# Chunk 2 of a layernorm, an MLP and a long convolution enters without transposes, and GpSimd makes each first tap product

## The chip, the cores and the metric

The kernel runs on one core of one Trainium2 chip. The metric is device time in microseconds (us), from the start of the program to its end. Engines are named as in the profile: PE is TensorE (PEld its weight loads), DVE is VectorE, ACT is ScalarE, POOL is GpSimd, SP is SyncE, which only issues DMAs here.

## The reference

A sequence of 2048 rows of 448 channels goes through two branches that are added to the input. Branch A is a short causal convolution of `k` (4 taps), a product with `v`, a long causal convolution per channel by FFT, and a gate. Branch B is a dense layer, Mish, and a dense layer back.

```python
def _A_ref(q, k, v, shift_k, ssm_k, ssm_D):
    ...
    for t in range(ks):
        k_shift = k_shift + k_pad[:, t:t + S, :] * shift_k[:, ks - 1 - t][None, None, :]
    kv = k_shift * v
    ...
    y = (lambda x, s, axes=(-2,-1): jnp.fft.irfft2(x, s=s, axes=axes))(y_f, (1, L), axes=(1, 2))[:, 0, :S, :]
    y = y + kv * ssm_D[None, None, :]
    return q * y

def _B_ref(x, w1, b1, w2):
    h = jnp.einsum("bsd,df->bsf", x, w1) + b1
    sp = jnp.log1p(jnp.exp(-jnp.abs(h))) + jnp.where(h > 0, h, jnp.zeros_like(h))
    act = h * jnp.tanh(sp)
    return jnp.einsum("bsf,fd->bsd", act, w2)

x = A_q
xn = _layernorm(x, axis=-1)
return x + _A_ref(xn, A_k, A_v, A_shift_k, A_ssm_k, A_ssm_D) + _B_ref(xn, B_w1, B_b1, B_w2)
```

## The kernel before, in words

**The MLP sets the beat.** The rows are cut into 8 chunks of 256 (numbered 0 to 7), the 1792 hidden features into 7 pairs of 128. One (chunk, pair) is a pair step, 56 in all, and each is two half steps. In the even half step of pair step i, `g1_mm` (line 556) multiplies the chunk's normalised, transposed rows by the first weights. In the odd one ACT applies Mish (line 564), ACT rounds the result to a high part `ach` (line 98), DVE makes the low part `acl` (line 99), and PE multiplies the pair step i-2 by the second weights (`g2_mm`, lines 588 to 590). Weights, rows and activations are split in such high and low parts, and three products replace one of full precision. Half step s therefore belongs to pair step s/2; chunk c starts at half step 14c.

**How a chunk enters.** `XH` and `XL` hold a chunk's normalised rows with channels on partitions. Chunks below `NT` are normalised in rows (`ln_stats`: statistics on DVE, lines 442 to 448; the power and the normalisation on POOL, lines 451 and 455), turned by PE transposes (line 508, four of 128x128 for each half `jj` of a chunk) and split (lines 520 and 518). Chunks from `NT` on come by another way. `xT_load` (line 470) loads rows that were transposed beforehand, as `xn`. `nt_stats` (lines 478 to 483) makes the statistics with six ACT instructions on the row-wise copy `qt` and two POOL instructions, and POOL stores them to DRAM (`MR`, line 486). `nt_row` (line 489, issued by SP) reads them back, spread over all partitions, into `con`; `nt_norm` (line 495) subtracts and multiplies on DVE; `nt_split` (lines 502 and 503) makes `XH` and `XL`. The half steps of these stand in `NT_AT`, `NT_SOON`, `NT_HOW` and `NT_STATS`. `con` and `xn` have one buffer each.

**The convolution lies between.** It is three stages of small DFT products. The first (`f1_mm`, line 166) takes 8 groups of the filter (`h`) and 8 groups of `kv`. Each is called a visit here: PE makes 16 small products into the two PSUM tiles `pq` and `pr`; ACT copies `pr` (line 172); DVE adds and subtracts (line 176, twice, "the folds"); the sums go to DRAM on the ACT queue (line 187). The next visit writes `pq` and `pr` again, so it needs the folds to be done. `H_AT` and `KV_AT` give each visit's half step. A group of `kv` is made by `taps`: product u of four (u = 0 on line 209 and u = 2 on line 202, whole groups; u = 1 and 3 on lines 212 and 214, two halves), each added to the sum (line 219), and the product with `v` (line 222). `taps(g, u)` is placed by the distance to the group's visit; u = 2 is already made by POOL (`taps_pool`), placed right behind the visit before. DVE makes u = 0. In this document kv0 to kv7 are the groups of `kv`, and h0 to h7 those of the filter.

**What sets the order.** It is written out by hand: `at(slot, ...)` puts work ahead of a half step's products and `after(slot, ...)` behind them. Every engine and every DMA queue goes through its list in that order, and waits on semaphores where it needs another's work. Nothing is rearranged. SP issues all loads of `k`, `v`, `hT`, `q`, the transposed rows, the rows of statistics and the stores of finished chunks (line 615) on one queue.

Of the kernel before, what the change touches and what calls it, by code (L numbers as in the profile page):

```python
# [14 lines left out]
S, D, F = 2048, 448, 1792  # L15
# [7 lines left out]

G2_LAG = 2
H_HEAD = 1
H_AT = {2: 6, 3: 9, 0: 12, 4: 16, 5: 20, 6: 26, 7: 32}
KV_AT = (24, 29, 34, 39, 44, 50, 56, 60)
POOL_H = {20: (0, 2)}
OCT_AT = (66, 3)
I2_AT = {100: ((6, 7, 0, 1), 92, (95, 97, 98, 99), (0, 2, 0, 1)),  # L30
         108: ((2, 3, 4, 5), 101, (104, 105, 106, 107), (0, 1, 0, 1))}
LATE = 2
NT = 3
NT_AT = {"q": -5, "x": -1, "stats": -2, "flush": 0, "row": (4, 8), "norm": (7, 10), "split": (8, 11)}
NT_SOON = dict(NT_AT, row=(4, 5), norm=(4, 7), split=(6, 8))
NT_HOW = {c: dict(NT_SOON) for c in (4, 7)}
NT_HOW[6] = dict(NT_AT, row=(4, 10), norm=(8, 11), split=(9, 13))
NT_HOW[7]["x"] = 0
NT_HOW[3] = dict(NT_SOON, q=-9, stats=-3, flush=-2)
NT_HOW[5] = dict(NT_AT, q=-8, stats=-4, flush=-2)  # L40
NT_STATS = {3: 27, 4: 41, 5: 53, 6: 70, 7: 82}
EVAC_SOON = 2,
G1_SOON = (69, 75, 81, 87, 89)
END = 288
# [6 lines left out]
def tile_kernel(ctx: ExitStack, tc, q, qT, k, v, sk, hT, sD, head, w1, w2, c_g, c_gi, c_i2, out):  # L51
    nc = tc.nc
    V = nc.vector
# [24 lines left out]
    E = dp.tile([NJ * 4, 64, D], F32, name="E")  # L78
    MR = {c: dp.tile([2, CH], F32, name="MR") for c in range(NT, NCHUNK)}

# [8 lines left out]
    def rs(c):  # L89
        return rstd[:, 2 * c:2 * c + 2] if c < NT else mv[:, 2 * c:2 * c + 2, 1]  # L90

# [29 lines left out]
    def dv(n=1):  # L121
        for _ in range(n):
            if drip:
                drip.pop(0)()
# [4 lines left out]
    def at(slot, fn, *args):  # L129
        plan.setdefault(int(slot), []).append((fn, args))  # L130

    def after(slot, fn, *args):
        plan2.setdefault(int(slot), []).append((fn, args))
# [4 lines left out]
    skb = sp1.tile([128, 4, D], F32, name="skb")  # L138
    HT, KR, VT, KV, PP, PS, ST, SD = {}, {}, {}, {}, {}, {}, {}, []

    def xt():
        return sp1.tile([128, 2, D], F32, name="x", bufs=7)
# [61 lines left out]
    def taps(g, u):  # L204
        if (g, u) in PP:
            o = PP.pop((g, u))
        elif u % 2 == 0:
            o = xt()
            V.tensor_mul(o, KR[g - u // 2], skb[:, u:u + 1].to_broadcast([128, 2, D]))
        else:  # L210
            o = xt()
            V.tensor_mul(o[:, 0], KR[g - (u + 1) // 2][:, 1], skb[:, u])
            dv()
            V.tensor_mul(o[:, 1], KR[g - u // 2][:, 0], skb[:, u])
        dv()
        if u == 0:
            KV[g] = o
        else:
            V.tensor_add(KV[g], KV[g], o)  # L219
            dv()  # L220
        if u == 3:
            V.tensor_mul(KV[g], KV[g], VT.pop(g))
            dv()
# [207 lines left out]
    def xn_tile():  # L431
        return mp.tile([128, 4, CH], F32, name="xn", bufs=1)

    def ln_parts(c):
        st = mp.tile([128, 2, 6], F32, name="bst", bufs=2)
        ve = mp.tile([128, 2], F32, name="ve", bufs=2)
        if c < NT:
            XN[c] = xn = xn_tile().rearrange("p a b -> p (a b)").rearrange("p (j d) -> p j d", j=2)
        eng = nc.gpsimd if 0 < c < NCHUNK - 1 else V

        def stats(jj):
            V.bn_stats(st[:, jj], Q[c][:, jj])

        def aggr(jj):
            V.bn_aggr(mv[:, 2 * c + jj], st[:, jj])

        def eps(a, b):
            V.tensor_scalar(ve[:, a:b], mv[:, 2 * c + a:2 * c + b, 1], EPS, None, op0=ALU.add)

        def power(a, b):  # L450
            nc.gpsimd.tensor_tensor(rs(c)[:, a:b], ve[:, a:b], mhalf[:, a:b], op=ALU.pow)

        def norm(jj):
            j = 2 * c + jj
            eng.tensor_scalar(xn[:, jj, :D], Q[c][:, jj], mv[:, j, 0:1], rs(c)[:, jj:jj + 1],
                              op0=ALU.subtract, op1=ALU.mult)

        def tail(a, b, copy=eng.tensor_copy):
            copy(xn[:, a:b, D:], xn[:, a:b, D - 64:D])

        return stats, aggr, eps, power, norm, tail, ve
# [60 lines left out]
    def ln_T(c, jj):  # L522
        if jj == 0:
            dv(len(drip))
            x_tiles(c)
        p = pg()
        transposes(c, jj, p)
        for lo in range(2):
            x_split(c, jj, p, lo)
# [87 lines left out]
    def mlp_slot(s):  # L617
# [3 lines left out]
        if half == 0:  # L621
            if i < n:
                c, p = pairs[i]
                if c + 1 < NT:
                    if p == 0:
# [9 lines left out]
        else:  # L635
            if i < n:
                c, p = pairs[i]
                if p == NP - 2 and c + 1 < NT:
                    ln_T(c + 1, 0)
# [14 lines left out]

    for g, t in H_AT.items():
        if g != H_HEAD:
# [10 lines left out]
    for g in range(-2, 0):  # L667
        at(12, k_load, g)
    for g, t in enumerate(KV_AT):
        d = t - (KV_AT[g - 1] if g else t - 6)  # L670
        at(t - d - (3 if g > 1 else 2), k_load, g)
        at(t - d - 1, v_load, g)
        for u in range(4):
            after(t - (2 if g else 1) - d + d * u / 4, taps, g, u)
        at(t, f1_mm, KV, g, "kv")
        if g + 1 < NO:
            after(t, taps_pool, g + 1, 2)
        after(t, f1_fold, g, "kv")
        (at if t % 2 or g == NO - 1 else after)(t + (3 if g < NO - 1 else 2), f1_out, Dkv, g, "kv")
# [43 lines left out]

    for c in range(NT, NCHUNK):
        at_ = NT_HOW.get(c, NT_AT)
        b = 2 * NP * (c - 1) + (1 if c < 5 else 0)
        at(b + at_["q"], ln_load, c)
        at(b + at_["x"], xT_load, c)
        after(NT_STATS[c], nt_stats, c)
        for jj in range(2):  # L730
# [30 lines left out]
    stats, aggr, eps, power, norm, tail, ve = ln_parts(0)  # L761
# [134 lines left out]
```

## Time and profile before

| | |
|---|---|
| time, median of 3 runs (lowest, highest) | 357.84 us (356.28, 359.15) |
| the profiled execution: its time, its span | 356.18 us, 354.4 us |
| PE busy | 349.8 us, 99% of the span |
| DVE, ACT, POOL busy | 282.1, 160.7, 72.6 us (80%, 45%, 20%) |
| moved by DMA | 83.27 MB |
| granted PE clock | 0.998 |

The profile is of one execution. Each row of a timeline gives the start, the duration, the engine, the line, the operation with out<-in, the size and the number of instructions; in square brackets stands idle time before it and what ended it. A group's row gives the number of instructions, the busy time in us with the mean in ns, and the idle time before them. All times of place below are us from the span's start. Between half steps 12 and 60 the PE takes about 2.5 us for a half step and 1.1 us for a visit.

### The profile page before, as it was taken

Reading aid. Unit: us, or ns where it says so; the run is one execution under the profiler, and the core shown is the slowest. Engines: PE = TensorE matmul, PEld = TensorE weight load, DVE = VectorE, ACT = ScalarE, POOL = GpSimd, SP = SyncE. Lnnn points to the kernel's source line nnn. Section 1 sums busy time; section 2 is a strip of 40 time slices with the busy share of each in tenths; the row PEclk is TensorE's granted clock in tenths of the full one; section 3 lists DMA queues with packets and bytes.
Section 4 is the critical chain, followed back from the end, with each engine's and each line's share of the span. In section 5 each row is a group of like instructions: output and inputs, shape, how many; then the busy total and the mean of one; then the engine's idle time right before and its main releaser. Section 6 shows DMA issues by size and latency. Waiting matters only on the chain.

```text
span 354.4 us, 7525 instructions
## 1 busy us (share of the span) xinstructions
PE 349.8 (99%) x3098; PEld 288.6 (81%) x3098; DVE 282.1 (80%) x375; ACT 160.7 (45%) x310; POOL 72.6 (20%) x85
## 2 busy tenths in 40 slices
PE   8999999999999999999999999999999999999996
PEld 2988888888888989889887568658757699979795
DVE  5899748998999998979539869868985963788943
ACT  5967552347343643364232732423724333354480
POOL 3046002822220250212000120110310116040030
PEclk9999999999999999999999999999999999999999
DMA  7999977848769356652969489679756467989076
GB/s 251 366 339 353 401 277 182 338 131 236 212 178 314 128 150 176 219 163 36 298 187 365 149 307 298 229 243 372 263 144 254 105 173 261 407 334 277 25 116 143
DMA packets 30835, 83.27 MB, mean 235 GB/s; under 512 B 3153, under 2 KB 15954, under 8 KB 30802
## 3 DMA queue, kind: packets, MB, share of 16 engines
q1 hardware_dynamic: 21986, 47.78, 39.8%
q0 software_dynamic: 4928, 22.95, 20.4%
q10 hardware_dynamic: 3888, 12.08, 12.5%
q8 instruction: 24, 0.39, 0.4%
q14 instruction: 9, 0.07, 0.1%
HBM read 54.34 MB, written 28.45 MB: 234 GB/s over the span
## 4 chain that ended last, share of the span: by engine, by line
PE 97%; DMA 1%; SPq 0%; DVE 0%; issue 0%
PE pg L556 24%; PE pg L590 13%; PE pg L588 13%; PE pg L589 13%; PE pa L556 6%; PE pq L556 5%; PE pq L166 4%; PE pa L310 3%; PE pr L556 3%; PE pr L255 3%; PE pq L255 3%; PE pp L556 2%; PE pa L255 1%; DMA x<-in_head_dram 1%; PE pp L364 1%; PE pb L556 1%
## 5 line engine op out<-in xcount | busy, mean ns | idle before, releaser
L588 PE MATMUL pg<-w2h,ach 128*128 128x448 f32 x222 | 80.7, 363 | 0.0
L590 PE MATMUL pg<-w2h,acl 128*128 128x448 f32 x222 | 80.6, 363 | 0.0
L589 PE MATMUL pg<-w2l,ach 128*128 128x448 f32 x222 | 80.5, 362 | 0.0
L99 DVE TENSOR_TENSOR acl<-a,ach 128x512 fp32r<-128x512 f32 x56 | 38.9, 694 | 33.0 <-ACT ach L98 32.8
L556 PE MATMUL pg<-XH,w1h 128*128 128x256 f32 x264 | 52.7, 283 | 0.0
L564 ACT ACTIVATE a<-pg,b1t 128x256 f32<-128x256 f32 x66 | 27.8, 472 | 51.8 <-PE pg L556 40.9
L556 PEld LDWEIGHTS pg<-XH,w1h 128*128 128x128 f32 x264 | 41.3, 188 | 8.2 <-issue 6.3
L588 PEld LDWEIGHTS pg<-w2h,ach 128*128 128x128 f32 x222 | 41.6, 187 | 4.4 <-issue 1.4
L589 PEld LDWEIGHTS pg<-w2l,ach 128*128 128x128 f32 x222 | 41.7, 188 | 2.4
L590 PEld LDWEIGHTS pg<-w2h,acl 128*128 128x128 f32 x222 | 41.7, 188 | 2.4
L556 PE MATMUL pg<-XL,w1h 128*128 128x256 f32 x264 | 42.9, 277 | 0.0
L176 DVE TENSOR_TENSOR st<-pq,st 128x896 f32<-128x896 f32 x32 | 34.9, 1089 | 4.8 <-ACT st L172 4.2
L98 ACT CAST ach<-a 128x512 fp32r<-128x512 f32 x56 | 34.8, 621 | 8.2 <-PE pg L589 6.7
L556 PEld LDWEIGHTS pg<-XL,w1h 128*128 128x128 f32 x264 | 35.9, 188 | 0.0
L556 PE MATMUL pg<-XH,w1l 128*128 128x256 f32 x198 | 33.5, 278 | 0.0
L202 POOL TENSOR_TENSOR x<-kr,skb 128x896 f32<-128x896 f32 x8 | 17.0, 2128 | 72.1 <-PE pr L166 25.7
L321 POOL DMA_DIRECT2D E<-qe x14 | 8.8, 631 | 92.7 <-ACT qe L264 92.7
L556 PEld LDWEIGHTS pg<-XH,w1l 128*128 128x128 f32 x198 | 27.6, 188 | 0.0
L219 DVE TENSOR_TENSOR x<-x 128x896 f32<-128x896 f32 x24 | 26.2, 1091 | 1.1 <-POOL x L202 0.4
L172 ACT COPY st<-pr 128x896 f32<-128x896 f32 x16 | 14.5, 908 | 15.9 <-PE pr L166 14.7
L564 ACT ACTIVATE a<-pa,b1t 128x256 f32<-128x256 f32 x16 | 6.7, 472 | 20.8 <-PE pa L556 20.7
L166 PE MATMUL pq<-x,con 32*64 32x448 f32 x128 | 15.9, 560 | 0.1
(191 smaller groups left out, 645.8 us busy)
## 6 DMA issues: line engine op xcount, KB each, us to landing
Dkv<-st ACTq DMA_DIRECT2D x16, 448.0 KB, 5.5
ah<-Dh SPq DMA_DIRECT2D x8, 896.0 KB, 8.4
av<-Dkv SPq DMA_DIRECT2D x8, 896.0 KB, 9.6
e<-E POOLq DMA_DIRECT2D x8, 896.0 KB, 7.3
E<-qe POOLq DMA_DIRECT2D x14, 448.0 KB, 7.1
kr<-in_k_dram SPq DMA_DIRECT2D x10, 448.0 KB, 6.0
Dh<-st ACTq DMA_DIRECT2D x10, 448.0 KB, 6.9
x<-in_v_dram SPq DMA_DIRECT2D x8, 448.0 KB, 6.3
```

The source lines that it names most:

```text
L98: nc.scalar.copy(h, raw)
L99: V.tensor_sub(l, raw, h)
L166: nc.tensor.matmul(ps[h][64 * jj:64 * jj + 64, b, :D], f1[rg:rg + 32], x[rg:rg + 32, jj], start=True, stop=True, tile_position=(rg, 64 * jj))
L176: f(st[:, n], e, st[:, 1])
L202: nc.gpsimd.tensor_mul(o, KR[g - u // 2], skb[:, u:u + 1].to_broadcast([128, 2, D]))
L219: V.tensor_add(KV[g], KV[g], o)
L255: nc.tensor.matmul(bk(p, r)[32 * t:32 * t + 32, :D], g[rs, t, c], a[rs, t], start=True, stop=True, tile_position=(64 * r, 32 * t))
L556: nc.tensor.matmul(ps[n], l, r, start=all(m[0] != n for m in seq[:n_]), stop=all(m[0] != n for m in seq[n_ + 1:]))
L564: nc.scalar.activation(a[:, n], ps[n], AF.Mish, bias=b1t[:, 2 * p + n:2 * p + n + 1])
L588: nc.tensor.matmul(ps, ah[:, n, cs], w2h[:, f], start=f == 0, stop=False)
L589: nc.tensor.matmul(ps, ah[:, n, cs], w2l[:, f], start=False, stop=False)
L590: nc.tensor.matmul(ps, al[:, n, cs], w2h[:, f], start=False, stop=f == NF - 1 or (f == NF - 3 and jj == 1 and c == NCHUNK - 1))
```

## The change

Four tables and one line change. Chunk 2 moves from the first way of entering to the second (`NT` goes from 3 to 2): it gets its own times in `NT_HOW[2]` and its statistics behind half step 15, and its 8 transposes, its DVE statistics and its POOL normalisation go. The u = 0 product of every `kv` group goes from DVE to POOL. The visits of `kv` stand at 24, 30, 36, 42, 46, 52, 56, 60 instead of 24, 29, 34, 39, 44, 50, 56, 60, and that of h7 at 38 instead of 32. What is placed by a visit (loads, taps, stores) moves with it.

```diff
-H_AT = {2: 6, 3: 9, 0: 12, 4: 16, 5: 20, 6: 26, 7: 32}
-KV_AT = (24, 29, 34, 39, 44, 50, 56, 60)
+H_AT = {2: 6, 3: 9, 0: 12, 4: 16, 5: 20, 6: 26, 7: 38}
+KV_AT = (24, 30, 36, 42, 46, 52, 56, 60)
...
-NT = 3
+NT = 2
...
+NT_HOW[2] = dict(NT_AT, q=-1, x=1, row=(3, 7), norm=(5, 9), split=(7, 10))
...
-NT_STATS = {3: 27, 4: 41, 5: 53, 6: 70, 7: 82}
+NT_STATS = {2: 15, 3: 27, 4: 41, 5: 53, 6: 70, 7: 82}
...
         elif u % 2 == 0:
             o = xt()
-            V.tensor_mul(o, KR[g - u // 2], skb[:, u:u + 1].to_broadcast([128, 2, D]))
+            (V if u else nc.gpsimd).tensor_mul(o, KR[g - u // 2], skb[:, u:u + 1].to_broadcast([128, 2, D]))
```

The changed file has one line more ahead of everything named above, so line 209 is its line 210, and so on.

DVE, from the folds of h5 (half step 20) to those of kv0 (half step 24). Before:

```order
L176 TENSOR_TENSOR st<-pq,st 128x896
L219 TENSOR_TENSOR x<-x 128x896
L99 TENSOR_TENSOR acl<-a,ach 128x512
L212 TENSOR_TENSOR x<-kr,skb 128x448
L214 TENSOR_TENSOR x<-kr,skb 128x448
L219 TENSOR_TENSOR x<-x 128x896
L222 TENSOR_TENSOR x<-x 128x896
L209 TENSOR_TENSOR x<-kr,skb 128x896
L99 TENSOR_TENSOR acl<-a,ach 128x512
```

The same place now:

```order
L177 TENSOR_TENSOR st<-pq,st 128x896 x2
L220 TENSOR_TENSOR x<-x 128x896
L496 TENSOR_TENSOR xn<-xn,con 128x4x128 x2
L100 TENSOR_TENSOR acl<-a,ach 128x512
L213 TENSOR_TENSOR x<-kr,skb 128x448
L215 TENSOR_TENSOR x<-kr,skb 128x448
L220 TENSOR_TENSOR x<-x 128x896
L223 TENSOR_TENSOR x<-x 128x896
L504 TENSOR_TENSOR XL<-xn,XH 128x4x128
L100 TENSOR_TENSOR acl<-a,ach 128x512
```

Two normalising instructions of chunk 2 now stand ahead of the rest of kv0 and wait for its row of statistics in `con`; the first tap product of kv1 has left the list.

SP's queue, from the load of `k` for kv0 (the first `kr` row) on. Before:

```order
L192 DMA kr<-in_k_dram 128x896
L196 DMA x<-in_v_dram 128x896
L615 DMA out_dram<-qt 128x896
L426 DMA qt<-in_q_dram 128x896
L152 DMA x<-in_hT_dram 128x896
L192 DMA kr<-in_k_dram 128x896
L196 DMA x<-in_v_dram 128x896
```

Now:

```order
L193 DMA kr<-in_k_dram 128x896
L471 DMA xn<-in_qT_dram 128x1024
L197 DMA x<-in_v_dram 128x896
L490 DMA con<-MR 128x256
L616 DMA out_dram<-qt 128x896
L427 DMA qt<-in_q_dram 128x896
L153 DMA x<-in_hT_dram 128x896
L193 DMA kr<-in_k_dram 128x896
L490 DMA con<-MR 128x256
L197 DMA x<-in_v_dram 128x896
```

The read of chunk 2's statistics (`con<-MR`) stands ahead of the store of chunk 0, of the load of chunk 3 and of the load of `k` for kv1; it can only be issued when the statistics lie in DRAM.

POOL, the last tap products, before:

```order
L202 TENSOR_TENSOR x<-kr,skb 128x896 x2
L481 TENSOR_SCALAR ve<-bst 128x2
L482 TENSOR_TENSOR mv<-ve,mhalf 128x2
L486 DMA MR<-mv 128x2x2
L202 TENSOR_TENSOR x<-kr,skb 128x896
```

Now, the last two rows being those of kv7:

```order
L203 TENSOR_TENSOR x<-kr,skb 128x896
L482 TENSOR_SCALAR ve<-bst 128x2
L483 TENSOR_TENSOR mv<-ve,mhalf 128x2
L487 DMA MR<-mv 128x2x2
L210 TENSOR_TENSOR x<-kr,skb 128x896
L203 TENSOR_TENSOR x<-kr,skb 128x896
```

The first tap product of kv7 (line 210) stands behind the statistics of chunk 5 and ahead of the third product (line 203).

## The prediction

> **What bounds the kernel now.** I read the page's busy times first, then PE's waits, then PE's timeline with the other engines beside it. The first row is the page's, the second is all that the waits of PE answer.
>
> ```profile
> PE 349.8 (99%) x3098; PEld 288.6 (81%) x3098; DVE 282.1 (80%) x375; ACT 160.7 (45%) x310; POOL 72.6 (20%) x85
> PE pg L747 <- DVE wz L743: 1.0, 1, 1.0
> ```
>
> PE is the bound, and it waits once, for 1.0 us at the start. So the change gains just what it takes off PE's list, and loses just what it makes PE wait. DVE, ACT and POOL count only where they end late for a product. The sum is made against the profiled execution, 356.18 us with a span of 354.4; the median of the runs shown is 357.84, 1.66 more, and their spread is 2.87. About 1% (3.6 us) is what a measurement of this kernel can tell from no change.
>
> **What PE loses: 8 transposes.** PE's products overlap, so their price is read from start to start: here first a passage without transposes and the same passage with them, from g1 to g2, then the same pair from a visit to g1.
>
> ```profile
> 66.56 0.62 PE L556 MATMUL pg<-XL,w1h 128*128 128x256 f32 x4
> 67.22 0.36 PE L589 MATMUL pg<-w2l,ach 128*128 128x448 f32 x1
> ...
> 69.98 0.54 PE L166 MATMUL pr<-x,con 32*64 32x448 f32 x2
> 70.45 0.62 PE L556 MATMUL pg<-XH,w1h 128*128 128x256 f32 x3
> ...
> 72.62 0.62 PE L556 MATMUL pg<-XL,w1h 128*128 128x256 f32 x4
> 73.08 0.60 PE L508 MATMUL pg<-con,xn 128*128 128x128 f32 x4
> 73.73 0.37 PE L589 MATMUL pg<-w2l,ach 128*128 128x448 f32 x1
> ...
> 76.50 0.54 PE L166 MATMUL pr<-x,con 32*64 32x448 f32 x2
> ...
> 77.38 0.60 PE L556 MATMUL pg<-XH,w1h 128*128 128x256 f32 x3
> ```
>
> 72.62 to 73.73 is 1.11 against 0.66 from 66.56 to 67.22: 0.45 for the first four. 76.50 to 77.38 is 0.88 against 0.47: 0.41 for the others. Together **0.86 us** less on PE. Moved visits keep their 16 products. Two of them (29, 39) leave the place between g1 and g2 for that between g2 and g1; by these rows a change of the kind of product costs 0.4 at most, so I bound the two at -0.4 to +0.4 and take 0, since PE meets the same three kinds either way. All other changes are free as long as nothing arrives late, and there are three places where something may.
>
> **The price of POOL beside DVE.** Eight u = 0 products leave DVE and come to POOL, and POOL's normalisation of chunk 2 goes.
>
> ```profile
> L209 DVE TENSOR_TENSOR x<-kr,skb 128x896 f32<-128x896 f32 x8 | 8.7, 1084 | 0.0
> L202 POOL TENSOR_TENSOR x<-kr,skb 128x896 f32<-128x896 f32 x8 | 17.0, 2128 | 72.1 <-PE pr L166 25.7 <-issue 25.5 <-DVE x L201 20.8
> L99 DVE TENSOR_TENSOR acl<-a,ach 128x512 fp32r<-128x512 f32 x56 | 38.9, 694 | 33.0 <-ACT ach L98 32.8
> ...
> 62.73 2.77 POOL L455 TENSOR_SCALAR xn<-qt,mv,rstd 128x448 f32<-128x448 f32 x1
> 63.84 1.05 DVE L99 TENSOR_TENSOR acl<-a,ach 128x512 fp32r<-128x512 f32 x1
> 66.05 2.78 POOL L455 TENSOR_SCALAR xn<-qt,mv,rstd 128x448 f32<-128x448 f32 x1
> 67.12 1.49 DVE L222 TENSOR_TENSOR x<-x 128x896 f32<-128x896 f32 x1
> ...
> 124.31 1.14 POOL L481 TENSOR_SCALAR ve<-bst 128x2 f32<-128x2 f32 x1 [3.36 <-ACT a L480]
> 124.31 1.09 DVE L222 TENSOR_TENSOR x<-x 128x896 f32<-128x896 f32 x1
> 156.94 0.19 POOL L481 TENSOR_SCALAR ve<-bst 128x2 f32<-128x2 f32 x1 [9.45 <-ACT a L480]
> ```
>
> DVE saves 1.08 a visit, POOL pays 2.13. But the two hold each other up. POOL's tiny L481 takes 0.19 with DVE idle, and 1.14 beside an L222 that ends at 125.40: it starts to work when DVE's instruction is over. The other way round, while POOL normalises 448 elements, DVE's L99 takes 1.05 instead of 0.69 and L222 1.49 instead of the 1.09 of the other L222 row: 0.36 and 0.40 more. A product on POOL reads two inputs of 896, four times as much, so my estimate is up to 4 x 0.36 = 1.4 of delay on DVE; the ends are 0 and POOL's whole 2.13. I take 1.1, between the estimate and no overlap and nearer the former: DVE then neither gains nor loses, and POOL starts up to 1.1 later.
>
> The Trainium skill, page "SBUF — State Buffer", section "Who interferes with whom", has a rule that speaks against this part: a DVE instruction with two SBUF inputs and a POOL instruction that reads SBUF exclude each other, and the later one is blocked for the other's whole instruction. The L481 row agrees; L99 beside POOL's 2.77 does not, as it lost only 0.36. By the rule DVE would lose 2.13 a visit, and the sum below would be +1.5 to +3.8 instead of -0.36.
>
> **Place 1: kv0, and what its new wait holds.** The normalising of chunk 2 stands ahead of kv0's last products on DVE and needs the row of statistics.
>
> ```profile
> L495 DVE TENSOR_TENSOR xn<-xn,con 128x512 f32<-128x512 f32 x20 | 13.9, 693 | 0.3
> ...
> 46.69 0.94 ACT L98 CAST w2h<-x 128x896 fp32r<-128x896 f32 x1
> 82.48 0.58 ACT L478 ACTIVATE a<-qt 128x448 f32<-128x448 f32 x1 [0.72 <-DVE st L176]
> 85.73 0.19 ACT L480 ACTIVATION_READ_ACCUMULATOR a<-qt,mv 128x1 f32 x1
> 88.03 0.84 POOL L486 DMA_DIRECT2D MR<-mv  x1 [0.29 <-POOL mv L482]
> DMA to landing us min/median/max: 3.5/5.8/7.0
> DMA to landing us min/median/max: 2.9/5.2/9.8
> ...
> 69.52 0.59 PE L166 MATMUL pq<-x,con 32*64 32x448 f32 x2
> ```
>
> (The two landing rows are those of the store of `MR`, L486, and of the read of the row, L489.) ACT's statistics start behind w2h's rounding, at 47.6, and take 3.4 (82.48 to 85.92): 51.1. POOL issues the store 2.1 behind them (85.92 to 88.03): 53.2. With the medians it lands at 59.0 and the row at 64.2; with the shortest times of both at 59.6. DVE gets there at about 63.8 (the end of the instruction ahead of L99). In time, kv0 then needs 1.4 (two L495) and what stood from 63.84 to 68.61 less the 0.76 that POOL's normalisation cost: 5.4, so it is ready at 69.2 against 69.52 at PE. With the medians it is ready at 69.6, 0.1 late. Nothing else hides this: before, 0.9 was free. The statistics also push h4's copy and folds back by 2.4; the next visit is some 10 us away, so that costs nothing.
>
> **Place 2: h6's visit, through SP's queue.** The read of the row waits on SP, and behind it stand the store of chunk 0, the load of chunk 3 (which needs that store to have landed, as it takes its buffer), h6 and the load of `k` for kv1.
>
> ```profile
> 55.66 0.35 SPq L615 DMA_DIRECT2D out_dram<-qt  x1
> 59.91 0.33 SPq L426 DMA_DIRECT2D qt<-in_q_dram  x1
> 60.76 0.42 SPq L192 DMA_DIRECT2D kr<-in_k_dram  x1
> kr<-in_k_dram SPq DMA_DIRECT2D x10, 448.0 KB, 6.0
> ...
> 73.50 1.09 DVE L176 TENSOR_TENSOR st<-pq,st 128x896 f32<-128x896 f32 x1
> 76.03 0.59 PE L166 MATMUL pq<-x,con 32*64 32x448 f32 x2
> ```
>
> Row issued at 59.0, store 59.4, load of chunk 3 4.25 later (55.66 to 59.91), `k` 0.85 behind it: 64.5, landed 70.5. POOL's u = 0 of kv1 then ends at 72.6 to 73.7. DVE's list has the sum of u = 1 (1.09) ahead of kv0's folds (2.2), and it needs that product: folds done at 75.9 to 77.0. PE wants `pq` at 76.03 - 0.45 = 75.6. So 0.3 to 1.4 late with the median store, and 0 (74.2 to 75.3 against 75.6) if it lands about 2 sooner, as the shortest (3.5) did. What kv0 loses is not lost again here.
>
> **Place 3: kv7, behind chunk 5's statistics on POOL.**
>
> ```profile
> 158.22 0.78 POOL L486 DMA_DIRECT2D MR<-mv  x1 [0.29 <-POOL mv L482]
> 160.05 1.09 DVE L219 TENSOR_TENSOR x<-x 128x896 f32<-128x896 f32 x1
> 167.33 1.09 DVE L222 TENSOR_TENSOR x<-x 128x896 f32<-128x896 f32 x1
> 169.34 0.59 PE L166 MATMUL pq<-x,con 32*64 32x448 f32 x2
> ```
>
> POOL is free at 159.0, its product ends at 161.1 to 162.2; DVE's sum stood at 160.05, so it and all behind it come 1.1 to 2.2 later, and kv7 ends at 169.5 to 170.6 against 169.34. The new list of ACT has the store of kv5 behind the statistics instead of ahead of them, which can give some tenths back: between 0 and 1.3 late.
>
> The other visits have more room: kv1 to kv5 come one to three half steps later (2.5 us each), kv6 where it stood.
>
> **The sum.** -0.86 on PE; places 1 to 3 cost 0 to 0.1, 0 to 1.4, 0 to 1.3; I take 0.5 for all, nearer their lower ends, as a wait at one place gives the later ones room. -0.86 + 0.5 = -0.36: 355.8 by the profiled execution, **357.5** by the median.
>
> **The rivals.**
>
> *All in time.* Row and `k` land with their shorter times, and POOL runs beside DVE. 357.84 - 0.86 = 357.0. For it: PE never waited. Against it: three rooms of less than 1 us.
>
> *DVE held for POOL's whole product.* At h6 the held instructions (L503, L99, L212, L214) and at kv7 (L212, L214) move by 2.13 instead of 1.1: 1.0 more than the upper ends at both, 2.4 and 2.3 of waits, -0.86 + 4.7 = +3.8 if both; at one of them +1.5, 359.3. For it the 1.14, against it the 0.36. This is what the rule quoted above from the Trainium skill's page "SBUF — State Buffer" would make of the time.
>
> *Slower: the row comes late.* Store at its longest, 7.0, lands at 60.2, and the row at its longest, 9.8, at 70.0: kv0 ready at 75.4, PE waits 5.9, and the sum is +5.0: 362.8. It decides from a row that lands at 68.6, where kv0 is 4.5 late. For it: the DMAs are busy there and SP's queue is one list. Against it: 9.8 was reached in a later, more crowded stage.
>
> *Faster by over 1%.* The slower runs shown would have to wait at kv3 or kv4, whose visits come later now, and by more than they differ (357.84 - 356.18 = 1.66, with 0.86: 355.3, still 0.7%).
>
> **Chances.** Forecast 0.50, all in time 0.23, POOL's whole product 0.14 (a quarter of it beyond 1%), late row 0.09 (nearly all beyond 1%), faster 0.04. Over 1% faster 0.04, within 0.84, over 1% slower 0.12. The range goes from the fastest run less the gain (356.28 - 0.86 = 355.4) to the rival at one place with 0.7 for the runs' spread (360.0).
>
> **What would show it.** No L508 row after 40 us, and PE from 72 to 78 shorter by 0.86. Right, if PE's waits are some tenths at kv0 (L166), h6 or kv7 and nothing else. The row's landing against 64, and the start of kv1's first product on POOL against 70.5, tell place 1 and 2. DVE's two-input instructions beside a POOL product tell 0.4 from 1.4 from 2.1. Wrong, if PE waits more than 2 us in all, or if it waits for `acl` or `XL`, which none of the three places foresees.

## The result: 5% slower

The changed kernel takes 375.47 us (375.2 to 377.1) against 357.16 for the kernel before on the same chip: a ratio of 1.052, with an interval of 1.0491 to 1.0548. That is 18.3 us more. An earlier comparison, made from its two fastest executions alone (370.41 and 371.69; three others took 376.28 to 379.2), gave a ratio of 1.0386 (1.0326 to 1.0446). Its profiled execution was one of 1228 us, so the profile shown here is that of the same kernel run again (375.39 us, span 373.6).

The page's rows of busy time and of the clock, in the changed kernel:

```profile
PE 355.4 (95%) x3090; PEld 291.8 (78%) x3090; DVE 289.9 (78%) x366; ACT 163.7 (44%) x320; POOL 84.7 (23%) x91
...
PEclk9999999999899996998999999999999999999999
```

PE has 8 instructions less and is busy 5.6 us more, and the clock row has an 8, a 6 and another 8 where before it has nines alone. PE's waits (in total, times, longest; `x L223` is the last product of the taps, `qt L596` the emptying of a chunk's sums, `st L177` the folds), without those of the start, and the windows of the span in which the clock was halved (bounds, length, PE busy, granted clock):

```profile
PE pq L167 <- DVE x L223: 7.8, 2, 4.3
PE pg L589 <- DVE qt L596: 4.1, 2, 3.4
PE pq L167 <- DVE st L177: 1.0, 1, 1.0
```

```profile
100.50:103.90 3.40, 3.14 (x9) 0.50 0.98 227
141.40:148.20 6.80, 6.05 (x36) 0.50 0.26 96
175.60:179.00 3.40, 3.40 (x25) 0.50 0.08 22
```

The sum of the loss is in these rows. The waits that were not there before are 7.8 + 4.1 + 1.0 = 12.9 us: two visits whose `kv` is late (kv4 at 137.9, 4.29, and kv6 at 171.9, 3.53), two emptyings of a finished chunk's sums that are late (chunk 0 at 56.4, 0.70, and chunk 1 at 97.38, 3.38), and h6's visit, which waits 1.00 for kv0's folds. PE then has 3.4 + 6.8 + 3.4 = 13.6 us at half the clock. The first of these windows begins 0.26 us ahead of the end of chunk 1's wait (97.38 + 3.38 = 100.76), the second 0.75 ahead of the end of kv4's (142.15), so 12.6 us of work run at half speed and 6.3 are lost. 12.9 + 6.3 - 0.86 for the transposes makes 18.3, the size of what was measured. It leaves out a wait of 0.4 at the start, for the first filter data; that wait is between nothing and 1.2 in the profiles of all kernels here, so the agreement to a tenth is chance.

What made DVE late stands in the rows of DVE and POOL side by side, at the emptying of chunk 1 (L596), at kv4 and at kv6:

```profile
96.59 2.54 POOL L210 TENSOR_TENSOR x<-kr,skb 128x896 f32<-128x896 f32 x1
...
97.11 2.96 DVE L220 TENSOR_TENSOR x<-x 128x896 f32<-128x896 f32 x1
...
100.00 1.14 DVE L596 TENSOR_TENSOR qt<-pg,qt 128x448 f32<-128x448 f32 x2
...
133.00 2.14 POOL L203 TENSOR_TENSOR x<-kr,skb 128x896 f32<-128x896 f32 x1
...
135.08 2.13 POOL L210 TENSOR_TENSOR x<-kr,skb 128x896 f32<-128x896 f32 x1
135.18 2.99 DVE L220 TENSOR_TENSOR x<-x 128x896 f32<-128x896 f32 x1 [1.33 <-POOL x L203]
...
139.88 1.09 DVE L220 TENSOR_TENSOR x<-x 128x896 f32<-128x896 f32 x1
141.00 1.09 DVE L223 TENSOR_TENSOR x<-x 128x896 f32<-128x896 f32 x1
...
171.80 3.55 DVE L223 TENSOR_TENSOR x<-x 128x896 f32<-128x896 f32 x1
...
172.32 2.08 POOL L210 TENSOR_TENSOR x<-kr,skb 128x896 f32<-128x896 f32 x1
```

An L220 takes 1.09 alone and 2.99 beside POOL's first tap product: POOL ends at 137.21, DVE 0.96 later. The same happens to kv6's last product, 3.55 instead of 1.09, beside the first tap product of kv7 (there DVE's row begins 0.52 ahead of POOL's, and it ends 0.96 behind it all the same), and once at every one of the eight products; the lengthened instructions take 14.8 us more than their kind does alone, 1.85 for a product that saved DVE 1.08.

### The profile page after: what moved, and what is told of

It is laid out like the page before. It is cut to its first block, busy times and chain, and to the rows that moved or that the text cites. A ratio compares the mean times of both kernels' runs of the same rounds, so it can differ in the third digit from the quotient of the medians.

```text
span 1226.6 us, 7529 instructions
## 1 busy us (share of the span) xinstructions
PE 1222.5 (100%) x3090; PEld 830.9 (68%) x3090; DVE 281.5 (23%) x366; ACT 164.1 (13%) x320; POOL 80.2 (7%) x91
## 4 chain that ended last, share of the span: by engine, by line
PE 100%; DVE 0%; issue 0%
PE pg L557 25%; PE pg L591 13%; PE pg L589 13%; PE pg L590 13%; PE pa L557 6%; PE pq L557 5%; PE pq L167 4%; PE pa L311 3%; PE pr L557 3%; PE pr L256 3%; PE pq L256 3%; PE pp L557 2%; PE pa L256 2%; PE pp L365 1%; PE pb L557 1%; PE pg L748 1%
## 5 line engine op out<-in xcount | busy, mean ns | idle before, releaser
L591 PE MATMUL pg<-w2h,acl 128*128 128x448 f32 x222 | 222.2, 1001 | 0.0
L590 PE MATMUL pg<-w2l,ach 128*128 128x448 f32 x222 | 219.9, 990 | 0.0
L589 PE MATMUL pg<-w2h,ach 128*128 128x448 f32 x222 | 218.3, 983 | 0.0
L557 PEld LDWEIGHTS pg<-XH,w1h 128*128 128x128 f32 x264 | 125.0, 541 | 47.5 <-issue 44.9
L557 PE MATMUL pg<-XH,w1h 128*128 128x256 f32 x264 | 140.7, 652 | 0.0
L589 PEld LDWEIGHTS pg<-w2h,ach 128*128 128x128 f32 x222 | 103.0, 464 | 52.0 <-issue 51.9
L557 PE MATMUL pg<-XL,w1h 128*128 128x256 f32 x264 | 126.9, 654 | 0.0
L557 PEld LDWEIGHTS pg<-XL,w1h 128*128 128x128 f32 x264 | 122.6, 583 | 0.0
L557 PE MATMUL pg<-XH,w1l 128*128 128x256 f32 x198 | 97.3, 644 | 0.0
L557 PEld LDWEIGHTS pg<-XH,w1l 128*128 128x128 f32 x198 | 90.5, 573 | 0.0
L177 DVE TENSOR_TENSOR st<-pq,st 128x896 f32<-128x896 f32 x32 | 34.9, 1091 | 98.1 <-ACT st L173 97.3
L99 ACT CAST ach<-a 128x512 fp32r<-128x512 f32 x56 | 34.6, 619 | 36.7 <-PE pg L590 35.2
```

What stands on the lines that cost most here:

```text
L99: nc.scalar.copy(h, raw)
L177: f(st[:, n], e, st[:, 1])
L557: nc.tensor.matmul(ps[n], l, r, start=all(m[0] != n for m in seq[:n_]), stop=all(m[0] != n for m in seq[n_ + 1:]))
L589: nc.tensor.matmul(ps, ah[:, n, cs], w2h[:, f], start=f == 0, stop=False)
L590: nc.tensor.matmul(ps, ah[:, n, cs], w2l[:, f], start=False, stop=False)
L591: nc.tensor.matmul(ps, al[:, n, cs], w2h[:, f], start=False, stop=f == NF - 1 or (f == NF - 3 and jj == 1 and c == NCHUNK - 1))
```

## The experiments

Times of the kernel before in the five comparisons were 357.16, 356.65, 356.95, 356.91 and 357.06.

### Which part costs it

Three theories stood at first: a late row of chunk 2's statistics (A), DVE held by POOL's products (B), and the clock that PE loses behind a wait (C). The first run is the changed kernel as it is.

> The changed kernel once more, for a profile in which PE runs at its usual pace. Theory A (the late row of statistics, places 1 and 2): PE waits for 5 us or more at kv0's or h6's visit, near 70 to 76 us, and nowhere else. Theory B (DVE held by POOL's products): PE waits are spread over the visits or over acl, DVE's two-input instructions beside a POOL product take 0.7 to 2 us longer. Theory C (the clock): part of the 14 to 20 us is a granted clock under 1 behind a wait of PE. Time 370 to 379 us.

Measured: above. Then the changed kernel with the first tap products back on DVE:

```diff
-            (V if u else nc.gpsimd).tensor_mul(o, KR[g - u // 2], ...)
+            V.tensor_mul(o, KR[g - u // 2], ...)
```

> The change with the first tap products back on DVE; chunk 2's entry and the visits' places stay as changed. Theory A: still about 370 us, since the row is as late. Theory B: back to 356 to 358 us.

Measured: 364.33 us, ratio 1.0198 (1.018 to 1.0216). PE waits 2.37 at kv4 and 2.02 at kv6, each followed by 3.4 us at half the clock: 4.4 + 3.4 - 0.86 = 6.9 of the 7.2 lost. Neither theory has this time: POOL's products are worth 11.1 us of the 18.3, and 7.2 have another cause. Then the other way round, the kernel before with POOL's products alone:

```diff
-            V.tensor_mul(o, KR[g - u // 2], ...)
+            (V if u else nc.gpsimd).tensor_mul(o, KR[g - u // 2], ...)
```

> The kernel before with the first tap products on POOL, and nothing else changed. Theory A: 356 to 359 us. Theory B: slower by most of the loss, 365 us or more, with PE waiting at the visits of kv.

Measured: 363.98 us, ratio 1.018 (1.0155 to 1.0205): 6.8 us for this part alone, a little under what theory B gave. Last, the changed kernel with chunk 2 entering as before:

```diff
-NT = 2
+NT = 3
```

> The change with chunk 2 entering by transposes as before; first tap products on POOL and the visits' places as changed. Theory A: back to 356 to 358 us. Theory B: still 368 us or more.

Measured: 374.07 us, ratio 1.0467 (1.0444 to 1.0491), with the same waits at kv4 (4.37), kv6 (3.56) and chunk 1's emptying (3.40). Theory A falls as the main cause: 16.9 of the 18.3 us are there without chunk 2's row. What is left beside POOL's products is, in the main, the places of the visits.

### The places of the visits

> The kernel before with the visits' new places alone: h7 at 38, kv1 to kv5 at 30, 36, 42, 46, 52; no product moves to GpSimd, chunk 2 keeps its transposes. Theory V (a kv visit's room is its distance from the visit ahead, and the change makes two of them 4 half steps): TensorE waits 2.0 to 2.5 us at kv4 (half step 46) and about 2 us at kv6 (56), each is followed by 3.4 us at half the clock (1.7 us lost), and the time is 362.5 to 365, ratio about 1.02. Rival (the places cost nothing by themselves, the loss of the run with the products back on VectorE came from chunk 2's entry beside the new places): waits below 1 us each and 357 to 359, ratio 1.000 to 1.005.

```diff
-H_AT = {2: 6, 3: 9, 0: 12, 4: 16, 5: 20, 6: 26, 7: 32}
-KV_AT = (24, 29, 34, 39, 44, 50, 56, 60)
+H_AT = {2: 6, 3: 9, 0: 12, 4: 16, 5: 20, 6: 26, 7: 38}
+KV_AT = (24, 30, 36, 42, 46, 52, 56, 60)
```

Measured: 364.78 us, ratio 1.0234 (1.0208 to 1.0261). The wait of PE, and the window of half clock at its first part (the second has one of the same length, from 164.5):

```profile
PE pq L166 <- DVE x L222: 4.5, 2, 2.4
```

```profile
133.80:137.20 3.40, 3.38 (x23) 0.50 0.43 157
```

The waits are 2.39 at kv4 (half step 46) and 2.11 at kv6 (56); 4.5 and 3.4 for the clock make 7.9 of the 8.1 measured. The places alone cost this, with every product and chunk 2 as before. The last taps of a `kv` visit (from the third product on) stand in DVE's list behind the folds of the `kv` visit ahead, so its room is the distance to that one: kv4 now has 4 half steps instead of 5, kv6 4 instead of 6.

But it is not the 4 half steps alone: kv7 has 4 before and after the change. In the run with the products on DVE, this stands ahead of kv4 (ACT, then POOL, then DVE):

```profile
124.92 0.19 ACT L481 ACTIVATION_READ_ACCUMULATOR a<-qt,mv 128x1 f32 x1
125.01 0.89 ACT L173 COPY st<-pr 128x896 f32<-128x896 f32 x1
...
127.30 2.14 POOL L203 TENSOR_TENSOR x<-kr,skb 128x896 f32<-128x896 f32 x1
...
129.47 1.09 DVE L220 TENSOR_TENSOR x<-x 128x896 f32<-128x896 f32 x1 [1.32 <-POOL x L203]
```

Chunk 4's statistics (ACT, behind half step 41) stand ahead of the copy of kv3's visit, which is now at 42: PE's products began at 121.1, the copy at 125.0. POOL's part of them and the store stand ahead of kv4's third product, for which DVE waits 1.32. So they were moved two half steps on.

```diff
-NT_STATS = {2: 15, 3: 27, 4: 41, 5: 53, 6: 70, 7: 82}
+NT_STATS = {2: 15, 3: 27, 4: 43, 5: 53, 6: 70, 7: 82}
```

> The changed kernel with the first tap products back on VectorE, as in an earlier run (364.33), and in addition chunk 4's statistics two half steps later, at 43, so that they no longer stand between kv3's visit at 42 and its copy on ScalarE, nor ahead of kv4's third tap product on GpSimd. Theory S (kv4 is late because of the statistics beside it): the 2.37 us wait at 46 falls below 1 us, its stretch at half clock goes, kv6's 2.02 us stay, and the time is 360 to 361, ratio 1.009. Theory V (4 half steps are too few for the taps of a visit, whatever stands beside them): the wait at 46 stays at 2 us or more and the time at 364. The statistics' own user (chunk 4's row) could become late instead: then TensorE waits on XL at chunk 4's first products.

Measured: 364.19 us, ratio 1.0218 (1.0199 to 1.0237). kv4 no longer waits at all, so 4 half steps are enough where nothing stands beside them; but the time is the same, since kv6 now waits 5.05 instead of 2.02. The rows of that run, from SP's queue (L490 is the read of chunk 4's row, L193 kv6's `k`), DVE and ACT, and PE's wait:

```profile
142.82 0.32 SPq L490 DMA_DIRECT2D con<-MR  x1
...
143.85 1.85 SPq L193 DMA_DIRECT2D kr<-in_k_dram  x1
...
149.97 1.09 DVE L210 TENSOR_TENSOR x<-kr,skb 128x896 f32<-128x896 f32 x1 [2.65 <-DMA kr<-in_k_dram]
...
152.42 0.62 ACT L503 CAST XH<-xn 128x512 fp32r<-128x512 f32 x1 [6.13 <-DVE xn L496]
152.95 0.90 ACT L173 COPY st<-pr 128x896 f32<-128x896 f32 x1
...
PE pq L167 <- DVE x L223: 5.1, 1, 5.1
```

This chain crosses all queues. The second row of chunk 4 waits on SP until DVE has used the first, kv6's `k` is issued behind it and comes 2.65 us late for DVE; behind that product stand chunk 4's norms (L496), for these ACT's rounding (L503) waits, and behind that on ACT stands the copy of kv5's visit, which PE had made at 147.1. The folds, and with them kv6's taps, are late by all of it. The test takes one link out:

```diff
-        at(t - d - (3 if g > 1 else 2), k_load, g)
+        at(t - d - (5 if g == 6 else 3 if g > 1 else 2), k_load, g)
```

> As the run with the products on VectorE and chunk 4's statistics at 43 (364.19), with one edit more: kv6's load of k is issued at half step 47 instead of 49, so that in SyncE's queue it no longer stands behind the second copy of chunk 4's row, which waits for VectorE's norm. There VectorE waited 2.65 us for that load, kv5's copy stood behind the same wait on ScalarE, and TensorE waited 5.05 us at kv6 and then had 6.8 us at half the clock. Theory (the load's place in the queue is the cause): TensorE's wait at kv6 falls by at least 2.65, to 2.4 or less, and the time to 358 to 361.5. Rival (4 half steps are too few for kv6's taps beside chunk 4's norms): the wait stays at 4 us or more and the time at 363 to 365.

Measured: 359.8 us, ratio 1.0071 (1.005 to 1.0092).

```profile
PE pq L167 <- DVE x L223: 2.0, 1, 2.0
```

The load's place in the queue was worth 3.0 us of wait and the halved clock around it: each against the kernel before in its own comparison, 7.5 us lost became 2.9. The 2.01 us that are left have no halved clock behind them in this run. So two entries on what stands beside the visits, with the visits where the change put them, bring the 7.2 us lost down to 2.9.

### What POOL's product holds

The first run of this kind takes POOL's second input away: the kernel before, with half of u = 0 on POOL as a product with a constant (the true tap is left out there), the other half on DVE.

```diff
-            V.tensor_mul(o, KR[g - u // 2], ...)
+            if u:
+                V.tensor_mul(o, KR[g - u // 2], ...)
+            else:
+                nc.gpsimd.tensor_scalar(o[:, 0], KR[g][:, 0], 0.5, 0.0, op0=ALU.mult, op1=ALU.add)
+                V.tensor_mul(o[:, 1], KR[g][:, 1], skb[:, 0])
```

> The kernel before with work of u = 0 on GpSimd, as in an earlier run (363.98), but in a form that reads one tile instead of two: GpSimd multiplies one half of the tile by a constant 0.5 (the true tap is left out there, so kv is another result), VectorE makes the other half's product as before. GpSimd is still busy for some 2 us at the same places and VectorE's add still waits for it. Theory B (GpSimd's product with two input tiles holds one VectorE instruction of two tiles to its end, 1.3 to 2.5 us each time): the excess of VectorE's instructions falls from 14 us to 4 us or less (0.36 each, as beside the norms), TensorE's waits of 80.3 and 141.4 us fall below 1 us and the time is 357 to 359. Rival (VectorE's adds come late because they wait for GpSimd, whatever it reads): the waits stay and the time is 362 to 364.

Measured: 357.2 us, ratio 1.0014 (1.0002 to 1.0025), and the lengthened instructions of DVE take 4.0 us more than alone, 0.33 to 0.43 each. But POOL's instruction took 0.88 us and not 2, so it left open whether the inputs or the length decide. The second run makes POOL work longer than the true product: both halves on POOL, the first one twice, each with the constant.

```diff
-            V.tensor_mul(o, KR[g - u // 2], ...)
+            if u:
+                V.tensor_mul(o, KR[g - u // 2], ...)
+            else:
+                for jj in (0, 1, 0):
+                    nc.gpsimd.tensor_scalar(o[:, jj], KR[g][:, jj], 0.5, 0.0, op0=ALU.mult, op1=ALU.add)
```

> The kernel before with the whole of u = 0 on GpSimd, in three instructions that read one tile each (both halves times a constant 0.5, the first half once more, so kv is another result). The run with one such instruction held VectorE only 0.36 us each time, but that instruction took 0.81 us and not 2.1; three of them keep GpSimd for about 2.4 us, longer than the true product's 2.13, and VectorE's list is that of the run with the true product (363.98). Theory B (a product of two input tiles holds a VectorE instruction to its end, its length is not what costs): each of the 24 instructions lengthens one of VectorE's by 0.4 us at most, VectorE saves 1.08 a visit against it, TensorE's waits stay below 1 us each and the time is 356.5 to 358.5. Rival (VectorE's adds come late because GpSimd takes over 2 us for what VectorE made in 1.08): TensorE waits at 78 and 176 us again, 1.3 to 2 us each, and the time is 361 to 364.

Measured: 358.64 us, ratio 1.004 (1.0024 to 1.0056). The same place in both runs, first with the true product (POOL, then DVE's second half of u = 3), then with three instructions of one input (there L214 is L218, L219 is L223); below each, PE's waits in the whole run without those of the start:

```profile
70.24 2.49 POOL L209 TENSOR_TENSOR x<-kr,skb 128x896 f32<-128x896 f32 x1
...
70.68 2.53 DVE L214 TENSOR_TENSOR x<-kr,skb 128x448 f32<-128x448 f32 x1
...
PE pg L556 <- DVE XL L518: 2.0, 1, 2.0
PE pg L588 <- DVE qt L595: 1.3, 2, 1.1
PE pq L166 <- DVE x L222: 1.3, 1, 1.3
```

```profile
70.06 2.37 POOL L213 TENSOR_SCALAR x<-kr 128x448 f32<-128x448 f32 x3
...
70.50 0.97 DVE L218 TENSOR_TENSOR x<-kr,skb 128x448 f32<-128x448 f32 x1
72.46 1.09 DVE L223 TENSOR_TENSOR x<-x 128x896 f32<-128x896 f32 x1 [0.99 <-POOL x L213]
...
PE pg L592 <- DVE qt L599: 0.5, 1, 0.5
PE pq L166 <- DVE x L226: 0.5, 1, 0.5
```

POOL works 2.49 and 2.37 us at the same place (the second row joins three instructions). Beside the true product DVE's 0.62 us become 2.53, and it ends 0.48 behind POOL; beside the three they become 0.97. DVE does wait for POOL's result then, 0.99, and it costs PE almost nothing: 0.5 and 0.5. So the rival falls: what costs is not that POOL's result comes later than DVE's own did, but that an instruction of DVE is held. By the three rows of waits and the one stretch at half clock the run with the true product loses 2.0 + 1.3 + 1.3 + 1.7 = 6.3 of the 6.8 measured. The run with the longer work lost 0.1 more than its theory allowed.

That two inputs are the reason, as theory B has it, is not shown. Here is the next place in the run with one short instruction (L223 is L219 there):

```profile
75.27 0.57 POOL L212 TENSOR_SCALAR x<-kr 128x448 f32<-128x448 f32 x1
...
75.33 1.44 DVE L223 TENSOR_TENSOR x<-x 128x896 f32<-128x896 f32 x1 [0.19 <-POOL x L202]
```

POOL ends at 75.84 and DVE at 76.77, 0.93 behind it; beside the true product at kv4 the same kind of DVE instruction ended 0.96 behind POOL. It is so all through: a held DVE instruction with an output of 896 elements ends 0.93 to 0.96 behind the end of the POOL instruction that holds it, one of 448 0.47 to 0.49, whether POOL reads one tile or two. So POOL's product with a constant holds DVE to its end as well. It is only over sooner, and with three short ones DVE gets in between them. Inputs, elements and the length of one instruction were changed together here, and the true product in short pieces was not run.

The normalisation (L455), from which the forecast took its price, fits this too, read with two rows of before that stand beside those of the forecast:

```profile
27.59 1.85 POOL L455 TENSOR_SCALAR xn<-qt,mv,rstd 128x448 f32<-128x448 f32 x1
...
62.74 1.10 DVE L219 TENSOR_TENSOR x<-x 128x896 f32<-128x896 f32 x1
```

The L455 at 62.73 took 2.77 us, 0.92 more than the one at 27.59, and DVE's L219 began with it: that reads as POOL being held first, as L481 was in the forecast's rows. And beside that form DVE's instructions end 1.16 us sooner against POOL's end than beside the other two, in every profile (L99 0.62 ahead of it instead of 0.54 behind, L222 0.21 ahead instead of 0.95 behind). So that form lets DVE go 1.16 ahead of its end, and an estimate from these rows is that it holds for at most 1.85 - 1.16 = 0.7 us. DVE's 0.36 would then be the last part of that. Why the rest of it does not hold DVE stays open.

### Chunk 2's entry

> The kernel before with one part of the change alone: chunk 2 enters without transposes, all visits and all products where they stood. The forecast's term: TensorE has 0.86 us less, and nothing else is late, so 356.3 from the 357.16 of the last comparison, ratio 0.998. Rival: what the whole change lost with this part (375.47 against 374.07 without it, 1.4 us) belongs to the part itself, by chunk 2's row of statistics or by three more operations on VectorE and ScalarE ahead of kv0's visit: then 358 to 359, ratio 1.003 to 1.005, with a wait of TensorE of about 1 us or more at the pairs of chunk 1 or at kv0.

```diff
-NT = 3
+NT = 2
...
+NT_HOW[2] = dict(NT_AT, q=-1, x=1, row=(3, 7), norm=(5, 9), split=(7, 10))
...
-NT_STATS = {3: 27, 4: 41, 5: 53, 6: 70, 7: 82}
+NT_STATS = {2: 15, 3: 27, 4: 41, 5: 53, 6: 70, 7: 82}
```

Measured: 358.34 us (356.75 to 360.98), ratio 1.0045 (1.0019 to 1.0072): slower where 0.86 less was forecast. The profiled execution, at 356.75 the fastest, shows the gain and where it goes. PE's timeline, and ACT's copy of h4's visit:

```profile
55.69 0.62 PE L557 MATMUL pg<-XL,w1h 128*128 128x256 f32 x4
56.38 0.47 PE L589 MATMUL pg<-w2h,ach 128*128 128x448 f32 x1
56.70 0.36 PE L590 MATMUL pg<-w2l,ach 128*128 128x448 f32 x1
...
73.07 0.62 PE L557 MATMUL pg<-XL,w1h 128*128 128x256 f32 x4
73.52 0.36 PE L589 MATMUL pg<-w2h,ach 128*128 128x448 f32 x1
73.72 0.36 PE L590 MATMUL pg<-w2l,ach 128*128 128x448 f32 x1
...
76.59 0.54 PE L167 MATMUL pr<-x,con 32*64 32x448 f32 x2
77.06 0.62 PE L557 MATMUL pg<-XH,w1h 128*128 128x256 f32 x3
```

```profile
50.97 0.18 ACT L481 ACTIVATION_READ_ACCUMULATOR a<-qt,mv 128x1 f32 x1
51.06 0.89 ACT L173 COPY st<-pr 128x896 f32<-128x896 f32 x1
```

73.07 to 73.72 and 76.59 to 77.06 are 0.65 and 0.47, where the same passages took 1.11 and 0.88: 0.87 less, as priced. But 55.69 to 56.70 is 1.01, where the same passage from g1 to g2 takes 0.66 (in the rows of before that the prediction shows first): 0.35 lost. The new statistics push h4's copy back to 51.06 (48.70 before), the folds behind it, and behind these on DVE the adds that empty chunk 0 (L596), for which PE's products wait. Further pieces of 0.2 at chunk 2's second split, at kv1 and at 97 take the rest. The same kernel once more:

> Chunk 2's entry alone, once more, for another profiled execution: the one at hand was the fastest of 11 (356.75, against a median of 358.34 and up to 360.98) and shows no wait of TensorE behind the start. Theory R (chunk 2's row or transposed load lands late in most executions): a profile of 358 or more shows a wait of 1 to 3 us at the first products of chunk 2 or at kv0, ended by XL, behind an idle VectorE that waits for the row. Theory S (statistics ahead of h4's copy): it shows the wait at about 57 us, ended by the adds that empty chunk 0's sums.

Measured: 358.16 us (357.3 to 361.22), ratio 1.0038 (1.0016 to 1.0059); again the profiled execution was the fastest, and again it shows no wait above 0.2 behind the start. So what the slower ones lose is not seen. The next four runs move parts of the entry.

```diff
-NT_STATS = {2: 15, ...
+NT_STATS = {2: 17, ...
```

> As the run with chunk 2's entry alone (358.34), with that chunk's statistics two half steps later on ScalarE, at 17, so that they stand behind the copy of h4's visit (half step 16) and not ahead of it. Theory S (3.4 us of statistics ahead of the copy make VectorE's folds and, behind them, the adds that empty chunk 0's sums late): the loss of 0.35 us between 47 and 58 us of the span goes, the times draw together, and the median is 355.8 to 357, ratio 0.997 to 1.001. Rival (the loss and the spread of 4 us belong to chunk 2's row and transposed load, through SyncE's queue): still 358 to 358.5, or more, as the row has less room now.

Measured: 365.41 us, ratio 1.0235 (1.0207 to 1.0263). The 0.35 at 56 are gone, and the row of statistics is late:

```profile
67.16 1.42 DVE L496 TENSOR_TENSOR xn<-xn,con 128x512 f32<-128x512 f32 x2 [3.10 <-DMA con<-MR]
...
PE pq L167 <- DVE x L223: 2.7, 1, 2.7
PE pq L167 <- DVE st L177: 1.7, 1, 1.7
```

kv0 waits 2.74, and 6.8 us at half the clock begin 0.6 ahead of the end of that wait: the mechanism that was blamed first for the change exists, two half steps away from where the change put the statistics. Then one half step sooner:

```diff
-NT_STATS = {2: 15, ...
+NT_STATS = {2: 14, ...
```

> As the run with chunk 2's entry alone (358.34 and 358.16 in two comparisons), with that chunk's statistics one half step earlier, at 14, ahead of the stores of h0's group in ScalarE's list; nothing else changes place on any engine. They run at about 43 to 46.5 us of the span instead of 47.7 to 51.2, so the row of statistics has about 4 us more room and the copy of h4's visit is not behind them. Theory R (the row's way has too little room in most executions, and the copy behind the statistics costs the rest): the times draw together within 1.5 us and the median is 355.7 to 356.5, ratio 0.996 to 0.999: TensorE's 0.86 us are then seen. Rival (the loss lies elsewhere in the entry: its transposed load, its norms or its splits on VectorE): 358 or more and a spread of 3 to 4 us again.

Measured: 361.31 us, ratio 1.0125 (1.0102 to 1.0149), both expectations missed on the cause. ACT waits for the chunk's own rows, and all of its list stands behind:

```profile
47.96 0.58 ACT L479 ACTIVATE a<-qt 128x448 f32<-128x448 f32 x1 [3.27 <-DMA qt<-in_q_dram]
...
PE pg L589 <- ACT w2h L99: 1.9, 1, 1.9
```

The load of `q` for chunk 2, issued at 34 to 36 us, takes 10.9 to 12.2 us in the traces. The last two runs issue it ahead of the tap's row and two loads of `k`, with the statistics at 15 and at 14.

```diff
-NT_HOW[2] = dict(NT_AT, q=-1, ...
+NT_HOW[2] = dict(NT_AT, q=-4, ...
```

> Chunk 2's entry alone, statistics at 15 as in the change, and chunk 2's load of q issued ahead of the tap's row and two loads of k in SyncE's queue (about 29 us of the span instead of 34.7). Theory Q (in slower executions ScalarE waits for that load, and its list behind the statistics is late): the times draw together within 2 us and the median is 356.3 to 357.3, ratio 0.998 to 1.001 (0.86 less on TensorE, 0.35 lost at 57 us for the copy behind the statistics). Rival (the loss is elsewhere, in the row's way or the norms): 358 or more and a spread of 3 to 4 us, as without this edit; or the loads that now come later (k, w2) make their own users late.

Measured: 358.56 us (356.96 to 360.17), ratio 1.0045 (1.0023 to 1.0068). The load was issued at 31.1 instead of 34.7 and landed after 7.2 us, and the median did not move and the spread hardly (3.2 us, where it was 4.2 and 3.9), so it is not what the slower executions wait for.

> The same with the statistics at 14. Theory Q: ScalarE's wait of 3.27 us for the load is gone, so are the 1.9 and 0.65 us that TensorE waited behind it at 52 to 55 us, and the median is 355.7 to 357. Rival (the statistics at 14 are in the way of the casts that follow whatever the load does): TensorE still waits about 2 us at 52 us and the time is 359 or more.

Measured: 357.56 us, ratio 1.0018 (1.0001 to 1.0034), between the two expectations: the waits of 1.9 and 0.65 us are gone. 11 of the 12 times lie between 356.59 and 358.02. This is the best of all that were tried with chunk 2's new entry, and it does not beat the kernel before. More room for the row, or the copy that is no longer behind the statistics, took most of the spread away; which of the two did, and what the slower executions with the statistics at 15 wait for, stays open, as each of their profiles was of one of the fastest.

## Why the prediction was wrong

The forecast was 357.5 us and "within 1%"; the change is 5.2% slower.

Two steps failed most, and a third made both dearer. By themselves the visits' places cost 8.1 us, POOL's products 6.8 and chunk 2's entry 1.2 and 1.7 (two comparisons); the rest of the 18.3, about 2 us, is there only when they come together.

**The places of the visits were not worked out.** This step failed: "The other visits have more room: kv1 to kv5 come one to three half steps later". A later half step is not room. The last taps stand behind the folds of the `kv` visit ahead, so the room is the distance between the two, and at kv4 and kv6 it shrank. None of the three places of the forecast was at kv4 or kv6; what moved against them, chunk 4's statistics and kv6's load behind chunk 4's row, was in lists that were not read there.

**POOL beside DVE was taken too cheap.** "I take 1.1 ... DVE then neither gains nor loses": DVE loses 1.85 for each product and saves 1.08. The estimate, 4 x 0.36, took 0.36 for the price of 448 elements, but by the rows above that was only the last part of a hold, and more than half of the 2.77 us beside it held nothing. POOL's product with a constant holds for its whole 0.56 us, and four times that, 2.2 as an estimate, is near the 2.1 of the true product; so the factor may have been right, and the row that it was put to was not. The rule of the Trainium skill, page "SBUF — State Buffer", section "Who interferes with whom", was weighed against this and set aside at 0.14. For POOL's product of two tiles the traces agree with it (2.53 instead of 0.62 at 70.68), and for the one with a constant too (0.97 there, ending 0.47 behind the POOL instruction that held it); for the normalisation only in part, since it lets DVE go 1.16 us ahead of its end. That it is the later one that is blocked does not hold of kv6's last product, whose row begins 0.52 ahead of POOL's. The rival built on it, *DVE held for POOL's whole product*, had the right mechanism and too small a price, +1.5 to +3.8, since it was carried only to h6 and kv7. By itself it costs 6.8: at chunk 2's low part, at the emptying of chunks 1 and 2 and at kv7, and in the whole change, where the visits have lost their room, 11.1.

**A wait was priced at its length.** All sums of the forecast count a late visit once. A wait of 2 us or more at PE costs up to 1.7 us again, since 3.4 us at half the clock follow it, and up to twice that where 6.8 us follow. The term is missing everywhere; it is 6.3 of the 18.3 us. The profile of before could not show it, since PE waited only at the start.

**The emptying of a chunk's sums was not in the list of users.** L596 stands in DVE's list, and PE's products of the next chunk need it. PE waited 3.38 us for it at 97.4, where an L220 held by POOL had come in front of it; with chunk 2 alone it lost 0.35. The step "the statistics also push h4's copy and folds back by 2.4; the next visit is some 10 us away, so that costs nothing" looked at the next visit only.

**What held.** PE is the bound and pays for every wait. The transposes were worth 0.87 (priced 0.86), though the entry gave them back. Place 1: kv0 was in time; the row landed at 62.1, where 64.2 was given. Place 2: h6 waited 1.00, inside the 0 to 1.4 given, but that was luck. `k` landed at 69.75 and POOL's product ended at 72.17, both sooner than forecast; the folds were late because chunk 2's L504, at 70.13, was held by that product (2.59 instead of 0.69), which is the rival's mechanism. Place 3: kv7 did not wait in the changed kernel, where kv6's wait had given it room, and waited 1.30 with POOL's products alone, the upper end; there too a held instruction stands ahead of it (L212 at 165.31, 2.78 instead of 0.62). The rival *Slower: the row comes late* did not happen here; it did when the statistics stood two half steps later, where DVE idled 3.1 for the row and kv0 waited 2.7. The sign given for a wrong forecast, more than 2 us of waits in all, is what the profile shows.

## What to carry to other kernels

Where work is hung on a visit, its room is the distance to the visit ahead, less all that other tables have put between: read each engine's list at every place that moves, not only at those that look tight. Work given to an idle engine is not free if its instructions hold those of the busy one; measure the pair of operations in the form that will be used, since the row of another form, read without what stood in front of it, gave a fifth of the true price. In a kernel whose TensorE is never idle, a wait of 2 us can cost nearly 4 (of the thirteen of 2 us or more here, twelve had the halved clock around their end), so two or three late instructions outweigh any product taken off the list.

## What the runs showed of the hardware

**Half the clock behind a wait.** In the profiles of all these runs PE waited fourteen times for 1.97 to 5.05 us. Thirteen of the waits had a stretch of 3.4 or 6.8 us at half the clock, which began between 2.7 us ahead of the wait's end and 1.1 behind it; one of 2.01 had none, nor had any of those from 0.5 to 1.9. The Trainium skill, page "TensorE: Matmul & The Clock Gate", section "What's actually happening", has the clock fall after at least one idle window of about 3.4 us, with windows that run freely. The length of the stretches agrees; the idle time needed does not, since 1.97, 2.02, 2.11 and 2.37 us were enough here.

**How long POOL holds DVE.** A POOL `TENSOR_TENSOR` of 2.1 us held one DVE instruction of two tiles to its end, up to 2.57 us more than alone. A `TENSOR_SCALAR` with constants, 0.56 us where nothing delays it, did the same, up to 0.36 more. A `TENSOR_SCALAR` with the row's mean and deviation (L455), 1.85 us where nothing delays it, let DVE go 1.16 us ahead of its end and cost it 0.24 to 0.41. Folds, which read one tile from PSUM and one from SBUF, were not lengthened beside POOL's third product: 1.09 as always.

**An execution of 1228 us.** PE had the same list (3090 instructions) and waited only 1.0 us in all, and was busy for 1222.5 us instead of 355.4. It came once, and nothing here shows why.
